# A four-batch attention and mixing kernel: the first batch's Fourier stage by head pairs, its channel stage by halves, the weight conversion re-timed

## Chip, cores and metric

The kernel runs on one core of one Trainium2 chip. The metric is device time in microseconds (us) of one execution; a profiled execution has a span besides, which is a little shorter than its time. PE is TensorE (PEld its weight loads), DVE is VectorE, ACT is ScalarE, POOL is GpSimd, SP is the engine that issues most DMAs.

## What is computed

Three blocks follow each other for four batches (8 heads, 576 tokens, head dimension 64, model width 512):

```python
# 1 attention with a learned decay, for each batch and head
scores = q @ k.T / 8 + cum[:, None] - cum[None, :]     # cum = cumsum(log f), causal
x = softmax(scores) @ v                                # heads joined: 576 x 512
# 2 Fourier mixing and a channel MLP of 2048 features
u = x + real(fft(fft(x, axis=tokens), axis=features))
un = (u - mean(u)) / sqrt(var(u) + 1e-6)
x = u + relu(un @ w_ch1) @ w_ch2
# 3 gated spatial MLP
h = relu(x @ w_in);  a, b = h[:, :512], h[:, 512:]
out = (a * (w_spatial @ norm(b) + b_spatial)) @ w_out
```

The weights arrive as 64-bit floats and are turned into pairs of 16-bit numbers (a high and a low part) on the chip. Every product is three matmul passes: high by high, high by low, low by high.

## The kernel before

**Stages.** Batch 0's attention and Fourier stage run alone at the start (`xfirst`, order in the list `START`). Then `mlp(b)` runs for each batch: `mlp1` is the channel MLP, `mlp2` the gated one. While `mlp(b)` runs, the attention and Fourier stage of batch b+1 (`xsteps`) is laid between its pieces: every piece of `mlp` yields a planned duration, and events with due times up to that point are emitted (`run`, L1176). The due times stand in the tables `LATER` and `SECOND`. In this part the order on PE is the order of emission; the other engines' orders are chosen by the scheduler from a timeline of its own. In `START` only SP's order is fixed by hand.

**Attention.** It goes by four head pairs. Each pair has `load`, `stack` (transposes of q and k, copies to 16 bits, DMAs into the operand tiles S1 and S2), `max` (row maxima, then `mc`, L576 to L583, which carries the negated maximum as two 16-bit numbers, transposed into S2), `score` (four groups of scores, exponentials, a high and a low part; `XPOOL` says for batch 0 which low parts POOL makes) and `pv` (the product with v, then the division that writes the pair's 128 columns of X).

**Fourier stage.** `fold_pair` adds and subtracts mirrored tokens on POOL as soon as a pair is done (L725). After the last pair `fold` does the same over mirrored features, twice, and `hilo` splits the result. `dft1` transforms over tokens (36 matmuls of 321 columns), `dft2` over features (36 matmuls of about 128 columns and 27 of one), then X is updated. `norm_tile` normalises one token tile of five, transposes it and splits it into `unT`, which `mlp1` reads. Tiles 0 and 1 are done in `START`, tiles 4, 3, 2 at due times from `NORM2`.

**Channel stage.** `mlp1` (L880) has 24 units: three token tiles of 192, and for each eight pairs of 128-feature groups. `first(u)` makes 24 matmuls from `unT` and W1, `second(u)` 24 from the result and W2, two units later. Token tile after token tile goes through all 2048 features, so that the first eight units need all of W1 and W2.

**Weights.** 44 blocks of 128 rows by 512 (`weight_list`: w0 to w15 for W1, w16 to w31 for W2, w32 to w39 for W_in, w40 to w43 for W_out). `load_w` (L333) takes each through a DMA of 512 KB into a ring slot, two ACT operations (L349, L351), two of DVE (L353, L354), a POOL product (L363), an ACT copy (L365) and a POOL subtraction (L366). For the blocks in `VSIGN` a third DVE operation (L358) stands for L351 and L363. Two pairs of temporaries are used in turn. `START` holds w0 to w15 in full and the DMAs of six later blocks; the other 28 blocks follow in `weights_left`, four blocks in each of the first three units of `mlp1(0)` and one in each later unit (`WSTEP`), then the spatial weights.

## Time and profile before

| what | value |
|---|---|
| median of 3 runs | 966.71 us (964.13 to 968.37) |
| profiled execution, its own time | 966.72 us |
| its span | 965.0 us |
| PE busy | 844.5 us (88%) |
| DVE, ACT, POOL busy | 595.8, 395.5, 267.0 us |
| mean granted PE clock | 0.941 of full |

The stages of the profiled execution, by the first matmul of each: batch 0's attention and Fourier stage 0 to 144.67 us; `mlp1(0)` 144.67 to 324.17; `mlp2(0)` to 397.73; `mlp1(1)` to 538.44; `mlp2(1)` to 613.38; `mlp(2)` to 812.98; `mlp(3)` to the end. The busy times are averages over stages that have different limits, so a stage is read by the stretches of busy time, clock and idle time in it, not by the totals of the table.

### The profile page before, as it was taken

How to read it: one execution, taken by the hardware profiler on the slowest of the kernel's cores; microseconds unless marked ns; L12 is line 12 of the kernel's file. 1: busy time of each engine (PE TensorE's matmuls, PEld its weight loads, DVE VectorE, ACT ScalarE, POOL GpSimd, SP SyncE). 2: the span in 40 equal slices, each digit the busy share in tenths (PEclk: the TensorE clock that was granted, in tenths of full speed). 3: DMA queues.
4: the chain of work that ended last, by engine and by line, in shares of the span. 5: the costliest groups of instructions: out<-in, count | busy, mean ns of one | idle time of the engine just before them, and what ended most of it. 6: DMA issues, size and time to landing. Idle time of an engine off the chain costs nothing.

```text
span 965.0 us, 22425 instructions
## 1 busy us (share of the span) xinstructions
PE 844.5 (88%) x9405; PEld 730.0 (76%) x9405; DVE 595.8 (62%) x1452; ACT 395.5 (41%) x694; POOL 267.0 (28%) x372
## 2 busy tenths in 40 slices
PE   3776336897899899899999999899999999999997
PEld 2655135787899677589999686699999587999874
DVE  4676878897854776575765865576574973133341
ACT  1856456766634244253334234243323334111132
POOL 4565888554610542000000550000000450000010
PEclk9897567898899999999999999999999999999999
DMA  6772336917220000622010003522100001000001
GB/s 150 211 234 76 115 97 171 224 42 189 93 59 18 20 2 21 159 63 64 5 36 2 1 2 74 122 58 63 38 3 2 1 2 44 2 2 2 1 1 55
DMA packets 75020, 60.89 MB, mean 63 GB/s; under 512 B 59869, under 2 KB 60263, under 8 KB 74791
## 3 DMA queue, kind: packets, MB, share of 16 engines
q1 hardware_dynamic: 74199, 58.13, 23.2%
q0 software_dynamic: 720, 1.33, 0.6%
q8 instruction: 74, 1.21, 0.5%
q14 instruction: 27, 0.22, 0.1%
HBM read 40.43 MB, written 4.83 MB: 47 GB/s over the span
## 4 chain that ended last, share of the span: by engine, by line
PE 58%; DVE 5%; DMA 2%; SPq 1%; issue 1%; ACT 1%; POOL 0%; ACTq 0%; DVEq 0%
PE ph L898 15%; PE acc L919 14%; PE vs L1063 6%; PE pu L990 5%; PE pvv L1004 4%; PE po L1081 3%; PE yps L778 1%; PE sc L619 1%; PE sc L623 1%; PE pv L686 1%; PE tr L869 1%; PE mxt L589 1%; PE pv L688 1%; PE pv L687 1%; DMA S<-a 1%; PE eo L811 1%
## 5 line engine op out<-in xcount | busy, mean ns | idle before, releaser
L898 PE MATMUL ph<-unT,W 128*128 128x192 f16 x2304 | 212.2, 250 | 5.1 <-DVE hT L905 2.7
L919 PE MATMUL acc<-hT,W 128*128 128x192 f16 x2304 | 205.3, 246 | 0.0
L898 PEld LDWEIGHTS <-W 128*128 128x128 f16 x2304 | 196.8, 100 | 11.2 <-issue 6.3
L919 PEld LDWEIGHTS <-W 128*128 128x128 f16 x2304 | 191.7, 98 | 0.1
L904 ACT ACTIVATE hT<-ph 128x384 f16<-128x384 f32 x96 | 46.9, 489 | 143.8 <-PE ph L898 143.4
L905 DVE SCALAR_TENSOR_TENSOR hT<-ph,hT 128x384 f16<-128x384 f32 x96 | 53.1, 553 | 82.3 <-ACT hT L904 82.1
L643 ACT ACTIVATE P<-sc 128x1024 f16<-128x1024 f32 (+1 forms) x64 | 53.8, 841 | 70.3 <-DVE sc L636 53.9
L657 DVE TENSOR_TENSOR P<-sc,P 128x1024 f16<-128x1024 f32 (+3 forms) x50 | 49.7, 993 | 30.1 <-ACT sc L655 29.1
L688 PE MATMUL pv<-vh,P 128*128 128x65 f16 (+2 forms) x480 | 59.3, 203 | 6.2 <-POOL P L653 6.2
L619 PE MATMUL sc<-S 128*128 128x256 f16 (+2 forms) x288 | 54.1, 249 | 10.8 <-DVE a L493 7.0
L686 PE MATMUL pv<-vh,P 128*128 128x65 f16 (+2 forms) x480 | 60.0, 205 | 2.9 <-DVE P L657 2.9
L976 POOL COPY tsc<-sc 128x2 f32<-128x2 f32 (+1 forms) x24 | 4.6, 213 | 206.8 <-DVE sc L948 206.5
L687 PE MATMUL pv<-vh,P 128*128 128x64 f16 (+2 forms) x480 | 59.3, 203 | 0.0
L495 POOL COPY a<-a 128x2 f16<-128x2 f16 x32 | 6.4, 207 | 187.1 <-ACT a L492 137.2
L1063 PE MATMUL vs<-WP,vn 128*128 128x288 f16 x448 | 56.5, 286 | 0.0
L623 PE MATMUL sc<-S 128*128 128x256 f16 (+2 forms) x288 | 55.1, 249 | 0.0
L688 PEld LDWEIGHTS <-P 128*128 128x128 f16 (+2 forms) x480 | 50.0, 110 | 6.7 <-POOL P L653 6.6
L1004 PE MATMUL pvv<-WI,unT 128*128 128x512 f16 (+1 forms) x240 | 54.7, 381 | 0.0
L687 PEld LDWEIGHTS <-P 128*128 128x128 f16 (+2 forms) x480 | 49.8, 110 | 3.5 <-issue 3.2
L686 PEld LDWEIGHTS <-P 128*128 128x128 f16 (+2 forms) x480 | 49.2, 108 | 3.6 <-issue 0.2
L1063 PEld LDWEIGHTS <-vn 128*128 128x128 f16 x448 | 43.6, 98 | 10.8
L990 PE MATMUL pu<-unT,WI 128*128 128x192 f16 x576 | 51.5, 250 | 0.0
(231 smaller groups left out, 1652.9 us busy)
## 6 DMA issues: line engine op xcount, KB each, us to landing
S<-a SPq DMA_DIRECT2D x96, 144.2 KB, 3.0
WI<-in_moe_w_ch_dram SPq DMA_DIRECT2D x16, 512.0 KB, 4.7
W<-in_moe_w_ch_dram SPq DMA_DIRECT2D x16, 512.0 KB, 4.3
a<-in_k_dram SPq DMA_DIRECT2D x32, 144.0 KB, 3.9
a<-in_q_dram SPq DMA_DIRECT2D x32, 144.0 KB, 3.7
vraw<-in_v_dram SPq DMA_DIRECT2D x16, 256.0 KB, 5.7
WP<-in_moe_w_in_dram SPq DMA_DIRECT2D x8, 512.0 KB, 3.6
out_dram<-ob SPq DMA_DIRECT2D x16, 256.0 KB, 2.9
```

The lines of the kernel that those rows point to most:

```text
L619: T.matmul(ps[:, j, c0:c0 + w], S2[s][:, j, QN + 128 * kt:QN + 128 + 128 * kt], qh, start=i == 0, stop=False,)
L623: T.matmul(ps[:, j, c0:c0 + w], S1[s][:, j, 128 * kt:128 * kt + 128], q1, start=False, stop=last and b not in PEMASK,)
L643: A.activation(out=pt[:, 0], in_=src, func=AF.Exp, scale=1.0 / 2048.0)
L686: T.matmul(ps[:n, j, o0:o0 + 65], hi, vh[:kk, 0, kt, h, :], start=(i == 0), stop=False)
L687: T.matmul(ps[:n, j, o0:o0 + 64], hi, vh[:kk, 1, kt, h, 0:64], start=False, stop=False)
L688: T.matmul(ps[:n, j, o0:o0 + 65], lo, vh[:kk, 0, kt, h, :], start=False, stop=(i == len(jobs) - 1),)
L898: T.matmul(ph[:, c, :], W1[:, a, kc, 128 * ff:128 * ff + 128], unT[:, e, kc, tok(t)], start=(c == 0 and kc == 0 and i == 0), stop=(c == 1 ...
L905: V.scalar_tensor_tensor(out=hT[:, 1], in0=ph, scalar=0.0, in1=hT[:, 0], op0=ALU.max, op1=ALU.subtract)
L919: T.matmul(acc[t][d // 2][:, d % 2, :], W2[:, a, ff, 128 * d:128 * d + 128], hT[:, e, c, :], start=(ff == 0 and i == 0 and d % 2 == 0), st ...
L990: T.matmul(ph[:, c, :], WI[:, a, kc, 128 * ff:128 * ff + 128], xT[:, e, kc, tok], start=(c == 0 and kc == 0 and i == 0), stop=(c == 1 and ...
L1004: T.matmul(pv[:n, :], xT[:, a, kc, 128 * i:128 * i + n], WI[:, e, kc, DM:2 * DM], start=(kc == 0 and j == 0), stop=(kc == 3 and j == 2),)
L1063: T.matmul(ps, vn[:kk, a, s, 128 * c:128 * c + 128], WP[:kk, e, s, tok], start=i == 0, stop=i == len(jobs) - 1,)
```

## The change

Six edits go together.

- **Fourier stage of batch 0 by head pairs.** `fold_pair` folds tokens in two operations (for pair 2 on DVE, else on POOL) and splits the result at once; `dft1_first` transforms a pair's 128 columns over tokens (18 matmuls of 321 columns for each pair, 72 in all); `dft2_first` transforms over features without a fold, by full tables of 257 and 255 columns (72 matmuls of about 256 columns), the first three pairs' part apart from the fourth's. The tables are 1 MB more of DMA, after `tab`.
- **Channel stage of batch 0 by halves.** `mlp1(0)` goes through three token tiles with 1024 features, then again with the other 1024. Six more additions to `uT` on DVE.
- **Weights.** The order of blocks is now w0 to w7 the first half of W1, w8 to w15 the first half of W2, w16 to w31 the second halves, then W_in and W_out. `START` holds w0 to w7 in full up to a mark `|`. The 180 steps of the other 36 blocks get due times from `WT`: steps 0 to 64 at -5.1 to 8.6 planned us of `mlp1(0)`, up to step 93 at 35.5, the last weight step at 87, then the 12 spatial steps. `VSIGN` has five blocks in place of three.
- **pv.** The division is three DVE operations over all five token tiles in place of twelve; the middle tile's matmuls use 128 columns of weights in place of 65.
- **mc.** Two DVE operations in place of three; the constant that they carried goes into the exponential's bias.
- **Due times.** `LATER`, `SECOND`, `NORM2`, `NORD` (tiles 2, 4, 3) and `XPOOL` (third low part of group 3 to DVE) have new values.

```diff
-R1, R2 = 4, 4
-VSIGN = (0, 1, 5)
+VSIGN = (0, 5, 14, 18, 43)
-WSTEP = (4, 3)
-NORM2 = (0, 2.838, 3.101)
+WT = ((0, -5.1), (64, 8.6), (93, 35.5), (198, 98.0))
+NORD = (2, 4, 3)
+NORM2 = (0.58, 3.602, 3.209)
-FOLDV = (1, 0, 1)
-XADDV = (4,)
+PARTV = (2,)
+XADDV = (0,)
-XPOOL = (3, 4, 4, 3)
+XPOOL = (3, 4, 4, 2)
...
+score3 w3 w2 score3 w3 w2 score3 part2 score3 score3 score3 tok2 w3 score3 score3 w2 score3 w2 w4
+w4 w4 score3 w4 w3 tok2 score3 score3 pv3 pv3 part3 w6 w5 w5 feat0 w5 w6 w6 part3 feat1 tok3 tok3
+feat0 w5 feat0 feat0 norm0 feat1 feat1 feat2 w7 w7 feat2 w7 norm0 feat2 feat1 w7 norm1 norm1 feat2
+norm0 w6 norm1 norm1 norm0 | w8 w16 w8 w8 w8 w13 w8 w18 w11 w9 w10 w17 w9 w12 w9 w9 w19 w10 w9 w15
...
-        mr = rp.tile([128, 2, 5], F32, name="mr", tag="mr")
-        V.tensor_scalar(
-            out=mr, in0=mcol, scalar1=-1.0 / 16384.0, scalar2=LOG16 * 2048.0 / 16384.0,
-            op0=ALU.mult, op1=ALU.add,
-        )
-        V.tensor_copy(mc[:, :, :, 30], mr)
-        V.tensor_tensor(mc[:, :, :, 31], mr, mc[:, :, :, 30], op=ALU.subtract)
+        V.tensor_tensor(
+            mc[:, :, :, 30], mcol, neg.unsqueeze(2).broadcast_to([128, 2, 5]), op=ALU.mult
+        )
+        V.scalar_tensor_tensor(
+            out=mc[:, :, :, 31], in0=mcol, scalar=-1.0 / 16384.0, in1=mc[:, :, :, 30],
+            op0=ALU.mult, op1=ALU.subtract,
+        )
...
+        po = ps[:, :, 0:325].rearrange("p j (t d) -> p j t d", d=65)
+        V.tensor_scalar(out=rc, in0=po[:, :, :, 64], scalar1=16.0e-9, scalar2=None, op0=ALU.add)
+        V.reciprocal(rc, rc)
+        V.tensor_tensor(
+            X[:, :, 2 * D * hp:2 * D * hp + 2 * D].rearrange("p t (j d) -> p j t d", j=2),
+            po[:, :, :, 0:64], rc.unsqueeze(3).broadcast_to([128, 2, 5, 64]), op=ALU.mult,
+        )
...
     def fold_pair(hp):
+        E = V if hp in PARTV else G
         c = slice(128 * hp, 128 * hp + 128)
+        for e, op in enumerate((ALU.add, ALU.subtract)):
+            E.tensor_tensor(XF0[:, e], X[:, 0:2, c], X[:, 4:2:-1, c], op=op)
+        yield
+        xh = XH0[hp % 2]
+        hilo(*(xh[:, o:o + 512].rearrange("p (e t n) -> p e t n", e=2, t=2) for o in (0, 512)), XF0)
+        r = len(TOK[2])
+        hilo(xh[:r, 1024:1152], xh[:r, 1152:1280], X[:r, 2, c])
+        yield
+    def dft1_first(hp):
+        xh = XH0[hp % 2]
+        p = xps("yps")
+        for eo, tb in enumerate((CT, ST)):
+            for t in range(3):
+                r = len(TOK[t])
+                for i, (a, e) in enumerate(PASSES):
+                    o = 512 * a + 256 * eo + 128 * t if t < 2 else 1024 + 128 * a
+                    T.matmul(p[:, eo, 0:321], xh[:r, o:o + 128], tb[e][:r, t, :],
...
+    def dft2_first(t):
+        for part in (range(3), range(3, 4)):
+            for k in part:
+                for eo, o, m in ((0, 0, 257), (1, 257, 255)):
+                    for i, (a, e) in enumerate(PASSES):
+                        T.matmul(p[:n, eo, eo:eo + m], YC0[:, k, a, eo, cs], TAB0[:, e, k, o:o + m],
...
+        ng = 2 if b == 0 else 1
+        nu = NFF // 2 // ng
+        units = [(g, t, nu * g + f) for g in range(ng) for t in range(3) for f in range(nu)]
...
+        nxt += [(float(np.interp(i, *zip(*WT))), f) for i, f in enumerate(wleft)]
```

## Rows read from the trace of the kernel before

**Rows 1.** The page: busy us, share of span, count; then the chain's shares
```profile
PE 844.5 (88%) x9405; PEld 730.0 (76%) x9405; DVE 595.8 (62%) x1452; ACT 395.5 (41%) x694; POOL 267.0 (28%) x372
PE 58%; DVE 5%; DMA 2%; SPq 1%; issue 1%; ACT 1%; POOL 0%; ACTq 0%; DVEq 0%
```

**Rows 2.** Stretches by stage: length, busy PE, PEld, DVE, ACT, POOL; clock, DMA share, GB/s
```profile
0.00:102.88 102.88, 59.68 (x721) 47.98 (x721) 66.59 (x143) 54.58 (x77) 57.64 (x66) 0.84 0.63 170
102.88:144.67 41.79, 16.05 (x115) 11.67 (x116) 33.90 (x70) 21.30 (x44) 36.66 (x40) 0.59 0.30 89
144.67:324.17 179.50, 156.45 (x1915) 146.47 (x1915) 133.21 (x261) 105.05 (x179) 84.94 (x88) 0.90 0.40 108
...
397.73:538.44 140.71, 135.08 (x1779) 128.54 (x1777) 90.73 (x268) 49.31 (x74) 4.29 (x16) 0.99 0.18 41
```

**Rows 3.** The same within `mlp1(0)`, and the first four units of `mlp1(2)` last
```profile
144.67:186.66 41.99, 28.72 (x244) 25.09 (x244) 35.38 (x52) 27.29 (x47) 30.22 (x28) 0.76 0.74 191
186.66:215.00 28.34, 26.97 (x375) 25.31 (x374) 28.02 (x53) 20.85 (x36) 15.38 (x13) 1.00 0.33 88
215.00:250.00 35.00, 27.34 (x292) 25.33 (x290) 25.10 (x49) 25.14 (x41) 19.68 (x20) 0.90 0.55 149
613.38:637.03 23.65, 23.05 (x250) 21.10 (x249) 17.84 (x49) 11.34 (x17) 0.37 (x2) 0.96 0.39 95
```

**Rows 4.** Stretches, line L366 alone (one for each converted weight block): POOL busy (count)
```profile
0.00:102.88 102.88, 8.12 (x6) 0.84 0.63 170
102.88:144.67 41.79, 9.48 (x8) 0.59 0.30 89
144.67:186.66 41.99, 13.61 (x11) 0.76 0.74 191
186.66:215.00 28.34, 5.95 (x6) 1.00 0.33 88
215.00:250.00 35.00, 10.29 (x9) 0.90 0.55 149
```

**Rows 5.** What PE waited for, 144.67 to 324.17 us: total us, times, longest
```profile
PE mxd L512 <- DMA S<-a: 7.0, 1, 7.0
PE mxt L589 <- DVE mc L583: 2.5, 1, 2.5
```

**Rows 6.** Timeline 95 to 141 us: start, us, engine, line, operation, count, idle before
```profile
95.72 0.16 DVE L696 TENSOR_SCALAR rc<-pv 128x4 f32<-128x4 f32 x1 [0.51 <-PE pv L688]
98.24 1.50 DVE L358 SCALAR_TENSOR_TENSOR WO<-W,WO 128x512 int32<-128x512 int32 x1
102.41 0.47 DVE L703 TENSOR_TENSOR X<-pv,rc 128x128 f32<-128x128 f32 x2
...
117.35 2.62 PE L778 MATMUL yps<-tab,xoh 128*128 128x321 f16 x9
123.65 0.82 DVE L785 SCALAR_TENSOR_TENSOR yc<-yps,yc 128x642 f16<-128x642 f32 x1
129.73 0.91 POOL L831 TENSOR_TENSOR X<-X,tt 128x256 f32<-128x256 f32 x1
140.34 1.09 PE L869 MATMUL tr<-cft,un 128*128 128x128 f32 x4 [12.19 <-DVE un L855]
```

**Rows 7.** Groups by line, of 144.67 to 324.17 us: busy us, mean ns
```profile
L388 PE MATMUL wpps<-cft,wps 128*128 128x128 f32 (+1 forms) x15 | 2.6, 273 | 0.0
L354 DVE SCALAR_TENSOR_TENSOR wt<-wt 128x512 int32<-128x512 int32 x4 | 2.8, 689 | 0.2
L354 DVE SCALAR_TENSOR_TENSOR WO<-WO 128x512 int32<-128x512 int32 x26 | 21.7, 840 | 2.8 <-ACT WO L349 2.6
L363 POOL TENSOR_TENSOR WO<-WO,W 128x512 f32<-128x512 f32 x18 | 24.0, 1335 | 20.0 <-DVE WO L354 11.2 <-DMA vraw<-in_v_dram 4.2 <-DVE mr L578 2.4
```

**Rows 8.** The same view for the mc line L582, 0 to 215 and 400 to 965 us
```profile
L582 DVE CAST mc<-mr 128x10 f16<-128x10 f32 x6 | 4.1, 679 | 0.2
L582 DVE CAST mc<-mr 128x10 f16<-128x10 f32 x8 | 1.5, 188 | 0.2
```

More of the change, by code (lines that the diff above doesn't have):

```diff
@@ L136 @@
+w41 w40 w40 w41 w41 w41 w43 w42 w42 w42 w42 w42 w43 w43 w43 w43
 """
@@ new lines, in dft2_first @@
+    def dft2_first(t):
+        X = state[0]["X"]
+        n = len(TOK[t])
+        cs = slice(128 * t, 128 * t + n)
+        p = xps("eo")
+        for part in (range(3), range(3, 4)):
+            for k in part:
+                for eo, o, m in ((0, 0, 257), (1, 257, 255)):
+                    for i, (a, e) in enumerate(PASSES):
+                        T.matmul(
+                            p[:n, eo, eo:eo + m], YC0[:, k, a, eo, cs], TAB0[:, e, k, o:o + m],
+                            start=k == 0 and i == 0, stop=k == 3 and i == 2,
+                        )
+            yield
+        es = rp.tile([128, 512], F32, name="es", tag="s2", bufs=NS2)[:n]
+        A.activation(out=es[:, 0:257], in_=p[:n, 0, 0:257], func=AF.Copy)
+        tt = rp.tile([128, 512], F32, name="tt", tag="s2", bufs=NS2)[:n]
+        for i, op in enumerate((ALU.subtract, ALU.add)):
+            V.tensor_tensor(tt[:, 256 * i + 1:256 * i + 256], es[:, 1:256], p[:n, 1, 1:256], op=op)
+        yield
+        for tl, a in ((t, 0), (4 - t, 1)) if t < 2 else ((2, 0),):
+            e = 1 - a
+            E = V if tl in XADDV else G
+            xt = X[:n, tl, :]
+            for xc, src in (
+                (slice(1, 256), tt[:, 256 * a + 1:256 * a + 256]),
+                (slice(511, 256, -1), tt[:, 256 * e + 1:256 * e + 256]),
+                (slice(0, 257, 256), es[:, 0:257:256]),
+            ):
+                E.tensor_tensor(xt[:, xc], xt[:, xc], src, op=ALU.add)
@@ L734, in fold @@
         r = len(TOK[t])
-        E = V if b == 0 and FOLDV[t] else G
+        E = G
         sp = state[b]["a"][:r]
@@ L828, in dft2 @@
             e = 1 - a
-            E = V if b == 0 and tl in XADDV else G
+            E = G
             xt = X[:n, tl, :]
@@ L952, in mlp1 @@
         todo = []
-        for u in range(3 * nu + 2):
-            if u < 3 * nu:
+        for u in range(len(units) + 2):
+            if u < len(units):
                 first(u)
@@ L1118, in xsteps @@
                 seqs[f"part{hp}"] = fold_pair(hp)
-        for t in range(3):
-            seqs[f"fold{t}"] = fold(b, t)
-        for c in range(2):
-            seqs[f"tok{c}"] = dft1(b, c)
-        for t in range(3):
-            seqs[f"feat{t}"] = dft2(b, t)
+                seqs[f"tok{hp}"] = dft1_first(hp)
+        if b:
+            for t in range(3):
+                seqs[f"fold{t}"] = fold(b, t)
+            for c in range(2):
+                seqs[f"tok{c}"] = dft1(b, c)
+        for t in range(3):
+            seqs[f"feat{t}"] = dft2(b, t) if b else dft2_first(t)
         for t in range(5):
@@ L1137, in at @@
                 t, n = t if isinstance(t, tuple) else (t, 1)
-                ev.append((t, lambda: [next(seqs[key]) for _ in range(n)]))
+                ev.append((t, lambda: [next(seqs[key], None) for _ in range(n)]))
         at("v", *L["v"])
@@ L1162, in xfirst @@
         seqs["decay"] = decay_rows()
+        seqs.update({"b" + k: g for k, g in second.items()})
         wl = weight_list()
@@ L1165, in xfirst @@
             seqs[f"w{i}"] = load_w(i, *w)
-        for key in START.split():
+        first, rest = START.split("|")
+        for key in first.split():
             next(seqs[key])
-        return seqs
+        return seqs, [lambda s=seqs[key]: next(s) for key in rest.split()]
     def mlp(b):
@@ L1179, in run @@
             evs.pop(0)[1]()
+    second = xsteps(1)
     with tc.manual_schedule(engines={mybir.EngineType.SP}):
-        left = xfirst()
-    def weights_left():
-        for i in range(28 + NFF):
-            if any(True for _ in [*left[f"w{i}"]]):
-                yield
-        yield from load_spatial()
-    lw = weights_left()
-    def wsteps(n):
-        for _ in range(n):
-            next(lw, None)
+        left, wleft = xfirst()
+    spatial = load_spatial()
+    wleft += [lambda: next(spatial, None)] * 12
     pool0.__exit__(None, None, None)
```

151 lines of the change are left out of this document (84 added, 67 removed), and 2 rows, old and new, of the table PV.

## The prediction

> **What bounds the kernel now.** I read the page's totals first, then stretches of busy time cut at the stages, then the same inside `mlp1(0)`, then the waits there and the timeline of the tail before it. The totals say PE: 844.5 of 965.0 us busy, and 58% of the chain that ended last is PE [rows 1]. The stages say where that holds. From `mlp1(1)` on PE has 135.08 of 140.71 us [rows 2], so there only less PE work would help. Up to 102.88 us (the last write of pair 3's attention into X) PE has 59.68 of 102.88. Between there and the first channel matmul at 144.67 it has 16.05 of 41.79 at a clock of 0.59, while POOL has 36.66 and DVE 33.90 [rows 2]: here the conversion of weights and the fold share POOL and DVE, and PE waits. `mlp1(0)` takes 179.50 us where `mlp1(1)`, with the same matmuls and no weights, takes 140.71 [rows 2]. Its first four units take 41.99 us against 23.65 for those of `mlp1(2)` [rows 3]. The change works on the first 324.17 us alone; the 73.56 of `mlp2(0)` (to 397.73, where the next stretch begins) and the 567.27 us behind it I leave as they are, since PE fills `mlp1` there [rows 2].
>
> **The attention of batch 0.** Added: three times 18 matmuls of `dft1_first` in front of pair 3. Nine of them take 2.62 us at the low clock [rows 6], so 18 take about 4.9, and 14.7 in all. PE is idle for 43 of 102.88 us [rows 2], which would hide all of it if it fell there; where it stands ahead of scores it delays the pair. I charge a fifth, 3 us; the ends are 0 and 10. The splits of parts (about 1.3 us of ACT and DVE for a pair) are paid by the shorter pv and mc. Conversions: before, 6 blocks are done by 102.88 us [rows 4]; after, w0 to w4 stand ahead of pv3 in `START`, so no more. The extra 1 MB of tables passes in about 5 us at the 190 GB/s of [rows 3] and falls behind `load2`; the DMA share of 0.63 [rows 2] leaves room, and its cost is 0 to 3 us. Removed: pair 3's division starts at 95.72 and ends at 102.88, because weight steps (L358, 1.50) and fold steps stand between its twelve operations [rows 6]. Three operations take about 1.2 us, so 97. With the 3 us, X is complete at about 100 (95 to 110).
>
> **The tail from X to the first unit.** Before, 41.8 us. After, step by step from [rows 6], for pair 3 alone: two POOL operations of 256 columns at 0.91, 1.8; split on ACT and DVE with the middle rows, 1.8; 18 matmuls, 4.9; two copies of 0.82 or a little less, 1.5; the fourth pair's part of two `feat` steps, 12 matmuls of 256 columns, by columns from the same 2.62 about 2.7 (the other three pairs' parts run while PE waits); `es` and `tt`, about 1.2; additions to X on POOL for tiles 4 and 1, five of 0.91 or less, 4.7 at most; statistics, a power, `un`, eight transposes at 1.09 for four, and the split, 5.8 (an estimate but for the transposes). That sums to 24.4. On the same engines three blocks are still to be converted (w5 to w7) in place of eight [rows 4]; a block is about 2.5 us of POOL and 1.5 of DVE [rows 7]. Some ten hand-overs that each meet half an operation of 0.8 to 1.3 us cost about 5. So 29 us (24 to 36), and the first unit starts at 129 in place of 144.67: 15.7 gained. The fold's DVE and POOL operations disappear with this; they were on the path, so what is late next is the token transform on a cold PE and POOL's additions.
>
> **`mlp1(0)`.** Its PE work at full clock: 135.1 as in `mlp1(1)`, plus transposes of three token tiles, about 5 [rows 6], plus 2.6 of spatial transposes [rows 7]: 143. The halves add no matmul; they add six additions on DVE, about 3 us. So before, 36.5 of 179.5 us are lost: 23.05 idle and 13.5 to the lower clock. The head (four units) loses 18.3 of it [rows 3], the rest 18.2. No wait for a converted block is among PE's; its waits are those of batch 1's attention, above all 7.0 for the operands' DMA and 2.5 for mc [rows 5], each queued behind weight steps on DVE, ACT or POOL.
> After, 36 blocks are left in place of 30. In the head, 64 steps, or 12.8 blocks, fall due before 8.6 planned us; before, 12 blocks in the first three units. The head is therefore not relieved: the same stack, DMA and maxima stand between its first two units. I take 16, two less for the shorter mc. In the rest, 23 blocks: six thinly over seven units, then 17 at 1.3 for a unit of 5.4 us (140.71 / 26), one in 4.1 us. At one in 4.7 us (6 blocks in 28.34) PE lost 1.4 us, 0.23 a block [rows 3, 4]; at one in 3.9 (9 blocks in 35.00) 7.7 idle and some 2.7 by clock, 1.2 a block [rows 3, 4]. Six at 0.23 and 17 at about 0.55 make 11. Load agrees: DVE has 133.2 plus 9 for six more blocks, 3 for additions, 2 for `VSIGN`, less 8 for pv and mc, 139 of 170, or 82%; it had 84% in the head and 99% up to 215 [rows 3]. So 143 + 16 + 11 = 170, against 179.5. Bounds: 151, if only the 7.0 and little else stays; 185, if the rest pays 18.2 times 23/19. The moved DMAs share SP's queue with the attention's operand DMAs: a weight DMA that waits for its slot holds those behind it, which is inside the 7.0 and 16 taken. POOL has 84.9 plus 15 less 4, 96 of 170, and is no bound.
>
> **Edits with one answer.** The middle tile's pv matmuls stream the same 65 columns, so their wider weights cost nothing. `XPOOL` moves one subtraction of about 0.8 us from POOL to DVE, both idle then for part of the time. The new due times of batches 1 to 3 move work that lies beside a full PE; I take 0, with 5 either way, and in those batches pv and mc shorten DVE only, which has 90.73 of 140.71 us there [rows 2].
>
> **A rule against it.** The mc operation L582 takes 0.679 us up to 215 us, while POOL is busy, and 0.188 after 400 [rows 8]; L354 takes 0.840 and 0.689 [rows 7].
> The Trainium skill, page "SBUF — State Buffer", section "Who interferes with whom", says that DVE and GpSimd share a port pair: a DVE operation with two inputs in SBUF waits for a whole GpSimd operation that reads SBUF, as does a copy in its fast mode. By that rule the two new mc operations, each with two SBUF inputs, can still be held, the head gets back nearer 1 us than 2, and closer packing lengthens DVE's own steps. The trace agrees with the lengthening; that the new form is held no run here shows yet.
>
> **Sum.** 129 + 170 + 73.6 + 567.3 = 939.9 us of span. The profiled execution's own time is 966.72, 1.7 over its span, and equal to the median of 966.71, so 941.6.
>
> **Rivals.**
> 1. *The spreading works fully.* Rest and head lose only 12: 155; X at 97 with the same tail, 126. 126 + 155 + 73.6 + 567.3 + 1.7 = 923.6. For it: 186.66 to 215 lost 1.4 us with six blocks and DVE full [rows 3]. Against it: 64 steps due at once.
> 2. *DVE and POOL crowd each other.* Six more blocks in the stage cost at the old price: 185 in place of 170, 956.6. For it: the lengthened L354 [rows 7], and 215 to 250 us, where nine blocks cost PE 10.4 [rows 3]. That rule of the Trainium skill would give the same.
> 3. *Slower: the units wait for their blocks.* The place is `second` of the second half, which needs w31, 24 blocks after the first unit, with nine units behind it. At r us for a block and a start 5 us early, the stage is 24r - 5 + 9 x 5.41. It reaches the 195.2 that undoes the gain of 15.7 at r = 6.3, and is slower by over 0.5% from 6.5; at 6.7 it is 204.5, and the time 976. Against it: 41.99 us for 11 blocks is 3.8, 28.34 for 6 is 4.7 [rows 4].
> 4. *No change: the tail doesn't shorten.* If the token transforms and eight blocks push pair 3 to 110 and the tail to 30, the first unit comes at 140; with 184 the time is 966.6.
>
> **How the numbers follow.** The forecast (928 to 954) has 0.52, rival 1 0.20, rival 2 0.16, rival 3 0.06, rival 4 0.06. Faster by over 0.5% (under 961.9; 0.5% is about what a measurement of this kernel can tell from no change) is the forecast, rival 1 and most of rival 2: 0.86. Same: rival 4 and the slow end of rival 2, 0.08. Slower: rival 3, 0.06. The range leaves out 0.06 below (a tail at its lower end together with rival 1) and 0.14 above: 914 to 961.
>
> **What would show it.** Right: the first `ph` matmul at 120 to 136 us; between X and it 24 to 36 us with about three L366; 36 L366 after it; the first four units in 36 to 42 us; the first `pvv` of batch 0 290 to 308 us in; the distance from there to the end within 5 us of 640.8. Wrong: PE waits named after L366 or L365 (rival 3); a first unit after 138 (rival 4); L354 over 0.9 us on average with a stage over 180 (rival 2); a head near 24 us (rival 1). The prediction fails most easily in the head, for which I took the old loss because the same steps crowd into it.

## The result, and the profile of the changed kernel

The changed kernel takes 973.25 us (median of 5 runs, 970.67 to 975.85) where the kernel before took 966.66 beside it (964.13 to 968.37): a ratio of 1.0062 with a 95% interval of 1.0033 to 1.009. The change makes it 0.6% slower. I had forecast 941.6 us in a range of 914 to 961.

The page's totals of the changed kernel answer [rows 1]:

```profile
span 974.1 us, 22331 instructions
PE 855.5 (88%) x9450; PEld 735.8 (76%) x9450; DVE 576.1 (59%) x1283; ACT 408.5 (42%) x693; POOL 258.6 (27%) x357
```

DVE has 169 instructions and 20 us less than before, as the diff says, and POOL 8 us less. PE has 11 us more, and 974.1 - 855.5 = 118.6 us idle against 120.5 before. So work was taken from the two engines that I had called crowded, and the span still rose by 9.1 us, nearly what PE got.

The stages follow, cut at the landmarks that the prediction used (last write of pair 3 into X, first `ph`, first `pvv` of batch 0, first `ph` of batch 1). They answer [rows 2]; the columns are the length of the stretch, each engine's busy time and instructions, the granted clock as a share of full speed, the DMA share and GB/s.

```profile
0.00:118.25 118.25, 74.08 (x801) 58.37 (x802) 77.23 (x121) 71.33 (x102) 67.30 (x70) 0.83 0.64 170
118.25:152.24 33.99, 13.81 (x83) 10.52 (x80) 22.75 (x43) 13.89 (x26) 24.40 (x30) 0.63 0.46 142
152.24:336.33 184.09, 156.79 (x1924) 145.63 (x1924) 127.72 (x235) 106.28 (x183) 82.36 (x90) 0.92 0.36 93
336.33:405.86 69.53, 64.74 (x520) 45.42 (x518) 45.10 (x113) 27.27 (x59) 22.59 (x44) 0.98 0.18 38
```

| stretch | before | forecast | after | after less forecast |
|---|---|---|---|---|
| attention of batch 0, to X complete | 102.9 | 100 | 118.25 | +18.25 |
| tail, X to the first unit | 41.8 | 29 | 34.0 | +5.0 |
| `mlp1(0)` | 179.5 | 170 | 184.1 | +14.1 |
| `mlp2(0)` and all behind it | 640.8 | 640.9 | 637.8 | -3.1 |
| span | 965.0 | 939.9 | 974.1 | +34.2 |

The attention gives 15.4 us more than before, `mlp1(0)` 4.6 more; the tail gives back 7.8 and the rest 3.1. That is the whole 9.1 us between the two profiled executions. So the question is why the attention got longer, and why the stage of the halves didn't get shorter.

**The attention.** PE's busy time up to X rose from 59.68 us [rows 2] to 74.08, by 14.4. Its idle time went from 43.2 to 44.2. The new PE work (9.1 us of `yps` matmuls and 3.0 of `eo` in that stretch) lay on top of the old idle time, none of it inside; and the 184 score matmuls take 22.8 us together in place of 18.3. PE's waits up to X in the kernel before, then in the changed one, say why; the columns are what waited for what, us in total, times, and the longest.

```profile
PE mxt L589 <- DVE mc L583: 9.6, 3, 4.7
PE mxd L512 <- DMA S<-a: 6.8, 2, 6.4
PE pv L688 <- POOL P L653: 6.2, 2, 5.6
PE pk L482 <- DMA a<-in_k_dram: 6.2, 2, 5.2
```

```profile
PE yps L773 <- ACT W L746: 14.6, 3, 7.2
PE mxt L629 <- DVE mc L620: 7.1, 3, 3.5
PE mxd L552 <- DMA S<-a: 5.8, 1, 5.8
PE pk L522 <- DMA a<-in_k_dram: 5.2, 1, 5.2
```

The longest entry of the changed kernel is new: three token transforms (L773) wait 14.6 us for the split of their pair (L746). The timeline around the first of them shows the queue at work (rows of PE, POOL, ACT and DVE; start, duration, and in brackets how long the engine sat idle and for what).

```profile
48.73 0.24 PE L728 MATMUL pv<-vh,P 128*128 128x65 f16 x1
...
49.95 0.82 DVE L737 TENSOR_TENSOR X<-pv,rc 128x640 f32<-128x640 f32 x1 [0.53 <-DVE rc L736]
...
51.28 1.45 POOL L755 TENSOR_TENSOR W<-X 128x256 f32<-128x256 f32 x2
...
54.36 0.67 ACT L388 ACTIVATE WO<-W 128x512 f32<-128x512 f32 x1 [3.24 <-DMA W<-in_moe_w_ch_dram]
...
55.47 0.63 ACT L746 ACTIVATE W<-W 128x512 f16<-128x512 f32 x1
...
56.16 0.72 PE L773 MATMUL yps<-tab,W 128*128 128x321 f16 x2 [7.18 <-ACT W L746]
...
56.67 0.37 PE L659 MATMUL sc<-S 128*128 128x193 f16 x1
```

Pair 0 is divided at 50.77, and POOL has its part done at 52.73. The split could start then, but in ACT's queue a weight step (L388) stands ahead of it and waits 3.24 us for its DMA. PE finished pv at 48.97, has the transform of pair 0 next in its queue, and stands for 7.18 us; behind it stand scores of pair 1 (L659), which then start without a wait of their own. The exponential of that group follows at 58.72.

The queue of ACT is the smaller part of the wait. Of the 7.18 us 1.8 pass until the division is done, 2.0 on POOL's part, 2.7 in ACT's queue and 0.7 on the split. The other two waits end at 75.75 (3.55 us) and 106.59 (3.82), and no step that waits for a DMA stands in them. The second has the split right behind POOL's part; in the third two exponentials stand ahead of the split for 1.5 us (rows of POOL, ACT and DVE):

```profile
73.62 1.41 POOL L755 TENSOR_TENSOR W<-X 128x256 f32<-128x256 f32 x2 [1.02 <-DVE X L737]
...
75.06 0.63 ACT L746 ACTIVATE W<-W 128x512 f16<-128x512 f32 x1 [0.31 <-POOL W L755]
...
102.72 1.71 DVE L755 TENSOR_TENSOR W<-X 128x256 f32<-128x256 f32 x2
...
105.91 0.63 ACT L746 ACTIVATE W<-W 128x512 f16<-128x512 f32 x1
```

So some 4 of the 14.6 us are the queue on ACT. The rest is the chain itself, division, fold and split, which PE sees in full because the transform follows its own pair at once.

**The blocks.** L405 ends the conversion of a block, as L366 did in [rows 4]; L405 by stretch (length, POOL busy and count, clock, DMA share, GB/s):

```profile
0.00:118.25 118.25, 11.95 (x10) 0.83 0.64 170
118.25:152.24 33.99, 7.36 (x6) 0.63 0.46 142
152.24:336.33 184.09, 34.01 (x28) 0.92 0.36 93
```

I had forecast at most 6 in the attention, 3 in the tail and 36 in the stage. It is 10, 6 and 28.

**`mlp1(0)`.** The first four units take 38.63 us, inside the 36 to 42 of the forecast. What the forecast doesn't have is the end of the stage. Its last 24.09 us in the changed kernel, and then the last 24.09 us of the same stage before:

```profile
312.24:336.33 24.09, 17.91 (x217) 15.94 (x216) 13.32 (x44) 9.09 (x28) 10.71 (x24) 0.79 0.14 37
```

```profile
300.08:324.17 24.09, 24.09 (x349) 23.77 (x347) 12.15 (x37) 8.47 (x22) 5.82 (x11) 1.00 0.10 26
```

PE is idle for 6.2 of 24.09 us there where it was full before, and its clock is 0.79 in place of 1.00. The timeline of PE in the changed kernel shows what stands there: four runs of spatial transposes (L427) close behind each other, with a wait for DVE ahead of the scores before them and ahead of three of the four.

```profile
318.40 0.19 PE L659 MATMUL sc<-S 128*128 128x65 f16 x1 [1.89 <-DVE WP L434]
...
319.20 0.49 PE L427 MATMUL wpps<-cft,wps 128*128 128x128 f32 x3
321.78 0.62 PE L427 MATMUL wpps<-cft,wps 128*128 128x128 f32 x2 [2.09 <-DVE P L697]
323.29 1.33 PE L427 MATMUL wpps<-cft,wps 128*128 128x128 f32 x5 [0.89 <-DVE WP L434]
325.93 0.58 PE L427 MATMUL wpps<-cft,wps 64*128 64x64 f32 x3 [1.31 <-DVE WP L434]
```

Before, the same transposes came one group every 2.3 to 6.5 us from 301.9 to 342.0 us, between units and the first steps of `mlp2(0)`.

### The profile page after: what moved, and what is told of

Same layout as the page of the kernel before. It is cut to its first block, busy times and chain, and to the rows that moved or that the text cites. A ratio compares the mean times of both kernels' runs of the same rounds, so it can differ in the third digit from the quotient of the medians.

```text
span 974.1 us, 22331 instructions
## 1 busy us (share of the span) xinstructions
PE 855.5 (88%) x9450; PEld 735.8 (76%) x9450; DVE 576.1 (59%) x1283; ACT 408.5 (42%) x693; POOL 258.6 (27%) x357
## 4 chain that ended last, share of the span: by engine, by line
PE 66%; DVE 14%; DMA 6%; ACT 6%; issue 3%; POOL 3%; SPq 2%; DVEq 0%; ACTq 0%; POOLq 0%
PE ph L989 16%; PE acc L1011 15%; PE vs L1158 6%; PE pu L1085 5%; PE pvv L1099 3%; PE po L1176 3%; PE pv L726 2%; DMA W<-in_moe_w_ch_dram 2%; PE sc L659 2%; DVE mcol L574 1%; PE mxt L629 1%; DMA S<-a 1%; PE tr L957 1%; PE sc L663 1%; DMA WP<-in_moe_w_in_dram 1%
## 5 line engine op out<-in xcount | busy, mean ns | idle before, releaser
L683 ACT ACTIVATE P<-sc,log 128x1024 f16<-128x1024 f32 (+1 forms) x64 | 59.4, 928 | 103.6 <-DVE sc L676 79.9
L697 DVE TENSOR_TENSOR P<-sc,P 128x646 f16<-128x646 f32 (+3 forms) x51 | 50.4, 989 | 46.4 <-ACT sc L695 46.3
L659 PE MATMUL sc<-S 128*128 128x256 f16 (+2 forms) x288 | 56.9, 257 | 9.7 <-DVE mcol L567 3.2
L726 PE MATMUL pv<-vh,P 128*128 128x65 f16 (+2 forms) x480 | 58.5, 204 | 2.5 <-DVE a L533 2.1
L663 PE MATMUL sc<-S 128*128 128x256 f16 (+2 forms) x288 | 58.8, 257 | 0.0
L728 PE MATMUL pv<-vh,P 128*128 128x65 f16 (+2 forms) x480 | 57.5, 202 | 0.0
L1099 PE MATMUL pvv<-WI,unT 128*128 128x512 f16 (+1 forms) x240 | 56.7, 392 | 0.0
L726 PEld LDWEIGHTS <-P 128*128 128x128 f16 (+2 forms) x480 | 47.5, 104 | 7.2 <-DVE a L533 2.4
L1085 PEld LDWEIGHTS <-WI 128*128 128x128 f16 x576 | 49.6, 101 | 1.4 <-issue 0.8
L728 PEld LDWEIGHTS <-P 128*128 128x128 f16 (+2 forms) x480 | 48.6, 106 | 0.7 <-issue 0.6
```

The source lines that it names most:

```text
L659: T.matmul(ps[:, j, c0:c0 + w], S2[s][:, j, QN + 128 * kt:QN + 128 + 128 * kt], qh, start=i == 0, stop=False,)
L663: T.matmul(ps[:, j, c0:c0 + w], S1[s][:, j, 128 * kt:128 * kt + 128], q1, start=False, stop=last and b not in PEMASK,)
L683: A.activation(out=pt[:, 0], in_=src, func=AF.Exp, scale=1.0 / 2048.0, bias=log16)
L726: T.matmul(ps[:n, j, o0:o0 + 65], hi, vh[:kk, 0, kt, h, :], start=(i == 0), stop=False)
L728: T.matmul(ps[:n, j, o0:o0 + 65], lo, vh[:kk, 0, kt, h, :], start=False, stop=(i == len(jobs) - 1),)
L1085: T.matmul(ph[:, c, :], WI[:, a, kc, 128 * ff:128 * ff + 128], xT[:, e, kc, tok], start=(c == 0 and kc == 0 and i == 0), stop=(c == 1 and ...
```

## The experiments

Theory A: a pair's token transform stands in PE's queue ahead of the next pair's scores and waits there for a split that is late. Theory B: the blocks converted early, inside the attention and the tail, make these longer. Theory S: the spatial steps came to stand in a bunch. Theory O came up on the way: the order in which the scheduler fills the queues of ACT, DVE and POOL is worth as much as any part of the change. All ratios are to runs of the kernel before on the same chip beside it, with their 95% interval; the other columns are from the profiled execution of each kernel, in us. One execution is a draw, too: the profiled one of tok_late took 982.85 us and that of tok_two_spatial 971.87, both 8 over their medians, that of tok_two 960.94, 3 under; and `mlp2(1)`, which the edit of tok_two doesn't touch, took 68.42 us in the changed kernel and 66.76 in tok_two.

| kernel | median | ratio | X complete | first `ph` | `mlp1(0)` |
|---|---|---|---|---|---|
| the kernel before | 966.7 | 1 | 102.9 | 144.7 | 179.5 |
| the changed kernel | 973.3 | 1.0062 (1.0033 to 1.0090) | 118.25 | 152.2 | 184.1 |
| pv_alone | 975.0 | 1.0079 (1.0055 to 1.0104) | 102.9 | 150.3 | 180.4 |
| halves_alone | 971.9 | 1.0050 (1.0025 to 1.0075) | 105.5 | 152.2 | 177.1 |
| four_alone | 976.7 | 1.0082 (1.0058 to 1.0106) | 129.9 | 163.9 | 172.9 |
| div_only | 976.3 | 1.0105 (1.0067 to 1.0142) | 101.4 | 149.2 | 183.6 |
| mc_bias_only | 974.6 | 1.0085 (1.0052 to 1.0118) | 108.2 | 157.7 | 173.3 |
| before_vsign | 974.4 | 1.0077 (1.0048 to 1.0105) | 102.7 | 148.2 | 184.8 |
| before_vsign2 | 971.0 | 1.0029 (1.0008 to 1.0050) | 101.4 | 145.7 | 184.6 |
| before_gate | 973.5 | 1.0083 (1.0057 to 1.0109) | 104.8 | 139.0 | 191.9 |
| after_gate | 985.9 | 1.0208 (1.0179 to 1.0236) | 118.5 | 148.5 | 197.7 |
| after_vsign | 981.1 | 1.0138 (1.0099 to 1.0177) | 122.7 | 158.6 | 183.5 |
| tok_late | 974.6 | 1.0062 (1.0036 to 1.0089) | 123.6 | 156.6 | 184.3 |
| tok_two | 964.1 | 0.9982 (0.9955 to 1.0010) | 112.65 | 145.1 | 179.9 |
| tok_two_vsign | 967.5 | 0.9993 (0.9971 to 1.0015) | 110.6 | 145.3 | 184.8 |
| tok_two_gate | 972.6 | 1.0074 (1.0047 to 1.0101) | 109.0 | 137.2 | 199.0 |
| tok_two_conv | 966.6 | 0.9989 (0.9971 to 1.0006) | 112.6 | 149.0 | 184.3 |
| after_spatial | 967.9 | 1.0001 (0.9977 to 1.0024) | 117.9 | 150.2 | 177.2 |
| after_spatial_vsign | 975.5 | 1.0077 (1.0048 to 1.0107) | 124.1 | 157.9 | 176.0 |
| tok_two_spatial | 964.1 | 0.9962 (0.9941 to 0.9983) | 113.6 | 147.8 | 179.8 |

### Each part alone, on the kernel before

**pv_alone**: the diff's edits to `attn_pv`, mc, the exponentials and `XPOOL`, nothing else.

> The kernel before with one part of the change alone: the middle token tile's pv matmuls with 128 columns, the division in three operations for all five tiles, mc in two operations on mcol, log 16 as the exponential's bias, and XPOOL's last entry 2. Fourier stage, channel stage and weight order stay as before. What I thought in the prediction: the division of pair 3 gets some 6 us shorter, so X is complete at about 97 in place of 102.88, and 960 to 964 us follow. Rival: the operations only change places with weight steps on the same engines, X stays at 102 to 104 and the time within 2 us of 966.7. Rival: the bias makes every exponential 0.09 us longer and ACT decides, 968 to 970.

1.0079: slower, and not in the stretch that I had named. X is complete at 102.9 as before; the tail takes 47.4 us in place of 41.8, with ten blocks converted in it in place of eight.

**div_only** and **mc_bias_only** take that part apart.

```
div_only:      only the PV table's third row (65 -> 128) and the division in three operations
mc_bias_only:  only neg, log16, mc in two operations and bias=log16
```

> The kernel before with the wider middle pv and the division in three operations alone (log 16 stays in mc's four operations). If pv_alone's 7 us come from the bias or mc: 960 to 967 us, X at 97 to 103. If they come from the division: 972 to 976 us.

> The kernel before with mc in two operations on mcol and log 16 as the exponential's bias alone; division and pv as before. If the bias (each exponential 0.09 us longer, 64 of them on the way to the end of mlp1(0)) or the two-input mc operations cost pv_alone its 7 us: 971 to 976 us. If not: 963 to 968 us. If each part by itself reshuffles the scheduler's order at a loss: both this and div_only over 969.

Each is slower by as much as both together (1.0105, 1.0085 and 1.0079), though div_only only replaces twelve DVE operations by three and widens one operand of pv. Two separate causes of 7 us should have added up. This is the case I had written last in the expectation of mc_bias_only, that any edit reshuffles the order at a loss. It became theory O.

**halves_alone**: the halves and the weight list in that order; START without the early DMAs of w18, w19, w32 and w33, and each later block's DMA two blocks ahead.

```diff
+            work = any(True for _ in [*left[f"w{i}"]])
+            if 16 <= i < 26 + NFF:
+                next(left[f"w{i + 2}"], None)
```

> The kernel before with the channel stage of batch 0 in halves of 2048 features and the weight list in that order, the blocks still converted one for each unit (four for each of the first three), each block's DMA two blocks ahead. Fourier stage, pv and mc as before. If the halves by themselves relieve mlp1(0): first unit unchanged at 143 to 147, the stage 170 to 175 in place of 179.5, 957 to 962 us. If the head with batch 1's stacks and maxima sets the stage and not the blocks' dates: the stage 177 to 182, 964 to 969 us. If the units wait for blocks at the second half: over 185, over 972 us.

1.0050. The stage takes 177.1, at the edge of the second case; the tail took 5.0 us more than before. The halves by themselves don't relieve the stage by the 9.5 us I had forecast; 2.4 is what the profile shows, with 29 blocks in the stage in place of 30.

**four_alone**: the Fourier stage by pairs in the kernel before.

```diff
-... pv0 w18 stack2 stack2 max1 pv0 max1 score1 score1 ...
+... pv0 w18 stack2 max1 pv0 max1 part0 part0 stack2 score1 tok0 tok0 score1 ...
```

> The kernel before with the Fourier stage of batch 0 by head pairs (parts, token transforms placed among the scores as in the changed kernel, no fold over features), the rest as before; w32 and w33 are fetched at the end of START, since their slots hold the transformed pairs. Theory A (a pair's 18 token matmuls stand in PE's queue ahead of the next pair's scores and wait there for POOL's parts and the split): X complete at 111 to 118, first unit at 144 to 152, 966 to 974 us. Theory B (what made the attention longer in the changed kernel is the ten blocks converted inside it, not the token transforms): X at 101 to 106, first unit at 131 to 138, 952 to 960 us.

1.0082, with X at 129.9, outside theory A's 111 to 118 and far from theory B's 101 to 106. PE waits three times for a split here as well, 16.8 us in all. Of the parts this one alone moves X far, by 27.0 us; pv_alone moves it by 0.0, halves_alone by 2.6. But ten blocks are converted before X, too, so this run doesn't clear theory B of its share. The tail (34.0) and the stage (172.9) are 7.8 and 6.6 us shorter than before.

### Where the order comes from: edits without work

The scheduler fills the queues anew for every kernel. So three kernels change only which block gets its sign on DVE.

```diff
before_vsign    -VSIGN = (0, 1, 5)            +VSIGN = (0, 1, 6)
before_vsign2   -VSIGN = (0, 1, 5)            +VSIGN = (0, 2, 5)
after_vsign     -VSIGN = (0, 5, 14, 18, 43)   +VSIGN = (0, 4, 14, 18, 43)
```

> The kernel before with VSIGN (0, 1, 6) for (0, 1, 5): the sign of block 6 in place of that of block 5 goes to DVE, no work is added or removed, PE's order is the same, and the scheduler puts ACT, DVE and POOL in another order in some hundred rows. Theory O (the order before is a favourable one among many near it, and any edit that reshuffles it costs 3 to 9 us): 970 to 976 us. Rival (the parts themselves cost): 964 to 969 us.

> The same with VSIGN (0, 2, 5): again no change of work; here PE's order changes too. Theory O: 970 to 977 us. Rival: 964 to 969 us.

> The changed kernel with VSIGN (0, 4, 14, 18, 43) for (0, 5, 14, 18, 43): no change of work, the queues reshuffled. If the changed kernel's order is as favourable as any near it: 973 to 982 us. If its 973 is a common draw: 966 to 980, either side, which would make the 0.6% between the two kernels a matter of the order drawn.

All three are slower than the kernel that they change: before_vsign by 0.77%, before_vsign2 by 0.29%, and after_vsign with 1.0138 against 1.0062. In before_vsign X comes at 102.7 as before; the tail took 3.7 us more and the stage 5.3. The order of either kernel is a favourable one among its neighbours, and a new draw costs about 3 to 8 us. Theory O is shown to that extent. It means that the losses of 0.5 to 1.05% of the parts alone can't be laid to the parts, and that the 0.6% between the two kernels is itself no larger than a draw. What moves by more, or moves the same way under two orders, can still be told.

### Theory B: the early blocks

**before_gate**, **after_gate**: w8 to w15 can't be fetched before the tail's first feature step.

```diff
+            if 8 <= i < 16:
+                V.tensor_copy(slot[:, 0:1], gate.bitcast(I32))
             nc.sync.dma_start(slot, src)
```

`gate` is a column that DVE copies from that step's result (from `y1` before, from `es` after).

> The kernel before with one edit: the DMA of each of w8 to w15 waits for a one-column DVE copy that needs the first feat step of the tail, so these eight blocks can't be converted ahead of it. Theory B (blocks that nobody needs yet stand in the queues of ACT, DVE and POOL ahead of the attention's and the tail's steps; 14 of them are done by the first unit, though it needs four): the tail shrinks from 41.8 us by 6 to 12, the first unit comes at 133 to 139, mlp1(0) pays some of it back, the whole 957 to 965 us. Theory A (the token transforms in PE's queue are what went wrong in the change): nothing here concerns them, the first unit stays at 143 to 147, and mlp1(0) gets longer by up to 8, 966 to 975 us.

> The changed kernel with the same gate on w8 to w15 (at the first es of the tail). Theory B: X complete at 108 to 114 in place of 117.4 (two blocks fewer inside the attention), the tail 24 to 29 in place of 34, first unit at 133 to 142, the whole 960 to 968 us. Theory A: X at 115 to 119, the tail 31 to 34, the whole 969 to 975 us.

Stretches of before_gate, then of after_gate (X, tail, stage):

```profile
0.00:104.78 104.78, 60.11 (x721) 48.21 (x721) 66.62 (x142) 53.02 (x74) 56.95 (x66) 0.86 0.57 152
104.78:139.00 34.22, 13.50 (x116) 10.50 (x117) 28.14 (x70) 14.49 (x31) 24.05 (x30) 0.65 0.41 127
139.00:330.90 191.90, 159.82 (x1915) 148.21 (x1915) 137.14 (x272) 114.37 (x194) 98.91 (x97) 0.87 0.39 107
```

```profile
0.00:118.46 118.46, 73.62 (x811) 56.88 (x811) 68.68 (x111) 63.05 (x88) 59.63 (x64) 0.87 0.51 126
118.46:148.50 30.04, 13.42 (x71) 10.18 (x72) 16.05 (x44) 10.47 (x20) 14.08 (x21) 0.68 0.55 194
148.50:346.20 197.70, 163.16 (x1925) 150.12 (x1925) 144.62 (x251) 118.23 (x203) 100.71 (x105) 0.88 0.40 107
```

Half of theory B holds: the tail shrinks, by 7.6 us and by 4.0. X doesn't move (118.46, though two blocks fewer lie ahead of it). And the stage pays more than the tail gave: 12.4 us with five blocks more in before_gate, 13.6 with seven more in after_gate; in tok_two_gate, below, 19.1 with seven. In before_gate this is no price of converting: PE's second products wait 10.0 us for blocks that come late, a wait that the kernel before doesn't have.

```profile
PE acc L924 <- ACT W L368: 7.4, 2, 5.5
PE acc L924 <- POOL W L369: 2.6, 2, 1.3
```

In after_gate and tok_two_gate no unit waits for a block, and the stage pays 1.9 and 2.7 us for each block more. So before_gate has theory B's first unit and theory A's time, and after_gate, at 985.9, lies above both. To fetch these eight blocks late is a loss on all three kernels.

**tok_two_conv** asks the same inside the attention: tok_two (below) with the DMAs of w0 to w4 behind the last stack.

> tok_two with the DMAs of w0 to w4 behind the last stack of batch 0, so that no block is converted in the first two pairs. If the blocks make the pairs longer: pair 1's write at 61 to 66 in place of 70, X at 103 to 108 in place of 112.6, the tail up to 8 longer, the whole within 4 of 964. If the token transforms' own work does it: X at 110 to 114.

Pair 1 comes at 65.7 in place of 70.0, as expected of the blocks; but by pair 3 it has all come back, X at 112.56 against 112.65, though eight blocks lie ahead of it in place of ten, and the time is 0.9989 against 0.9982. That is the second case: X follows the token transforms' own work. The two blocks lie in the tail now, which takes 36.4 us in place of 32.5.

### Theory A: the token transforms in PE's queue

**tok_late** moves the `tok` steps of pairs 0 to 2 in START to just ahead of the next pair's pv; **tok_two** moves `tok0` behind the scores of pair 2, `tok1` behind those of pair 3 and `tok2` behind pv of pair 3.

```diff
tok_two:
-... score1 w1 tok0 tok0 score1 ... max2 tok1 w5 tok1 score2 ... score3 tok2 w3 ... tok2 score3 score3 pv3 pv3 part3 ...
+... max3 tok0 tok0 pv2 max3 pv2 ... score3 score3 tok1 tok1 pv3 pv3 tok2 tok2 part3 ...
```

> The changed kernel with one edit: the token transforms of pairs 0, 1 and 2 stand one pair later, ahead of the next pair's pv and behind its scores; the same work, weights as they were. Theory A (PE's queue stands behind a token transform whose split is late): X complete at 103 to 109 in place of 117.4, the whole 960 to 967 us. Theory B (the ten blocks converted in the attention): X stays at 114 to 118, the whole 971 to 975 us.

> The changed kernel with the token transform of pair 0 behind the scores of pair 2, that of pair 1 behind the scores of pair 3, that of pair 2 behind pv of pair 3: the split of each is then some 20 us old. Theory A: PE's waits for a split (15.5 us in the attention) fall under 4 us, X complete at 104 to 109, the tail 1 to 4 us longer, the whole 963 to 969 us. Theory B: the waits move to scores and pv, X at 113 to 118, the whole 970 to 976 us.

tok_late gained nothing: 1.0062, as the changed kernel, and X at 123.6 is outside both ranges. Its trace has a reason: one pair's scores are too short a way. POOL has the part of pair 0 done at 52.08, but the split's step L746 comes at 59.42, behind weight steps and four exponentials on ACT, and PE, done at 51.46 with the scores and maxima ahead of it, waits 8.7 us for it in front of pv of pair 1. Such waits up to X sum to 12.1 us in place of 14.6, and those for mc to 16.7 in place of 7.1. tok_two goes further. PE's waits up to X in tok_two:

```profile
PE mxt L629 <- DVE mc L620: 13.2, 3, 7.5
...
PE yps L773 <- DVE P L697: 5.2, 2, 3.5
```

No transform waits for a split any more up to there (5.2 us are waits that end with a P subtraction of DVE); part of it went to the next link, mxt for mc (7.1 to 13.2). X comes at 112.65, 3.7 us after my expected 104 to 109, and the time is 964.1, within the expected 963 to 969. Of the 15.0 us between the two profiled executions 5.6 lie in the attention, 1.5 in the tail, 4.2 in the stage, and 3.7 behind it, where the edit moves nothing.

**tok_two_vsign** repeats it under the order of after_vsign.

> tok_two under the reshuffled order of after_vsign (VSIGN 0, 4, 14, 18, 43), to be held against after_vsign (981.1 us, 1.0138 of before). If the token transforms' place is a cause of its own: 6 to 12 us under it, 969 to 975 us, and PE's waits for a split in the attention under 4 us. If tok_two's gain was a favourable draw: 977 to 983 us.

967.5 us: 0.9993 against after_vsign's 1.0138. PE's waits for a split from 40 to 125 us, in after_vsign and then in tok_two_vsign:

```profile
PE yps L773 <- ACT W L746: 20.2, 4, 7.0
```

```profile
PE yps L773 <- ACT W L746: 2.0, 1, 2.0
```

So moving the transforms up to two pairs later gains 0.8% under one order and 1.4% under another, X comes 5.6 and 12.1 us earlier, and the wait that theory A names is gone or nearly so in both, while edits without work only lost. By these two pairs of runs the place of the transforms is a cause. How much of the gain is the new draw is open.

**tok_two_gate** has both this and the gate.

> Both edits together. If A and B each hold a part: X at 98 to 105, the tail 25 to 31, first unit at 124 to 135, the whole 948 to 960 us. If only one of them acts, no better than the better of the two alone. If neither, 969 to 976 us.

1.0074: X comes at 109.0, 3.7 us before tok_two's, with two blocks fewer ahead of it; the tail is down to 28.2 us and the first unit at 137.2, and the stage takes 199.0. What the gate adds to tok_two is a loss, as on the other two kernels.

### Theory S: the spatial steps

**after_spatial** and **after_spatial_vsign** give the twelve spatial steps later due times.

```diff
-WT = ((0, -5.1), (64, 8.6), (93, 35.5), (198, 98.0))
+WT = ((0, -5.1), (64, 8.6), (93, 35.5), (180, 87.3), (192, 121.0))
```

> The changed kernel with the dates of the twelve steps for the spatial weights alone changed: one every 2.8 planned us up to 121 in place of all by 94, so that their transposes lie among the last channel units and the first steps of mlp2(0), as before the change. Theory S (the steps came to stand in a bunch at the end of the stage, where PE has 13.82 of 20 us at a clock of 0.74): mlp1(0) 175 to 179 in place of 184.1, mlp2(0) up to 3 longer, the whole 964 to 969 us. Rival (PE would wait there anyway, for batch 1's attention): within 2 of 973.

> after_spatial under the same reshuffled order. If the bunch of spatial steps is a cause of its own: 4 to 7 us under after_vsign, 974 to 977 us. If it was a draw: 979 to 983 us.

967.9 us, 1.0001 against 1.0062, and under the other order 1.0077 against 1.0138: 0.6% each time. The stage shrinks by 6.9 and 7.5 us, and `mlp2(0)` takes 3.1 and 3.3 more. The last 24.09 us of the stage in after_spatial, beside the row of the changed kernel above:

```profile
303.30:327.39 24.09, 19.81 (x279) 19.09 (x277) 13.80 (x37) 7.13 (x17) 5.47 (x10) 0.93 0.05 14
```

PE is busy for 1.9 us more and its clock is 0.93 in place of 0.79. For the changed kernel theory S holds under both orders.

**tok_two_spatial** has both cures.

> Token transforms two pairs later (as in tok_two) and the spatial steps spread (as in after_spatial). If theories A and S are separate: 9 less from A and 5 to 8 from S, 954 to 960 us, faster than both kernels. If S is no cause: 962 to 966 us.

964.1 us, 0.9962 (0.9941 to 0.9983): the only kernel here that is faster than both, by 0.4% than the one before. It isn't the 954 to 960 that two separate gains would give. From tok_two (0.9982) it can't be told apart. The last 24.09 us of the stage in tok_two, then in tok_two_spatial:

```profile
300.94:325.03 24.09, 17.77 (x231) 16.03 (x230) 13.53 (x44) 10.41 (x32) 10.64 (x24) 0.86 0.13 37
```

```profile
303.47:327.56 24.09, 19.82 (x278) 19.04 (x277) 13.74 (x37) 7.17 (x17) 5.47 (x10) 0.93 0.05 14
```

So the end of the stage is relieved here as in after_spatial. But the stage as a whole takes 179.8 us in place of 179.9, in an execution that was 8 us over its median where tok_two's was 3 under; I have no run that says where the gain went.

## Why the prediction was wrong

**The token transforms.** "I charge a fifth, 3 us" was the step that failed worst. I took 43 us of idle PE for room. The idle time was there [rows 2], but it was made of waits (above all 9.6 us for mc, 14.2 for DMA and 8.2 for the subtractions behind the exponentials), each ahead of a step that the next one needs, and the transforms were put on that chain. PE's busy time to X rose by 14.4 us and idle time by 1.0: nothing was hidden. That 14.4 comes close to the 14.7 that I had added up is luck: the transforms took 9.1, the rest is feature steps and slower scores. "The ends are 0 and 10" didn't hold the result of 15.4 either. Two pairs later (tok_two) the wait for a split is gone, and X still comes 9.8 us later than before, with 12.7 us more of PE and 3.0 less idle. So 5.6 of the 15.4 went with the place of the transforms. The other 9.8 stayed; no run has the transforms with only the six blocks of the kernel before, so what part of it the blocks have is open.

**The splits of parts.** "Paid by the shorter pv and mc" counts busy time. The split is 1.3 us of work, but with the division and the fold it is a hand-over for which PE stands in front of each transform, 14.6 us in all, some 4 of them because other steps are ahead of it in ACT's queue. I had written of waits behind weight steps for `mlp1(0)` and not for this place.

**The blocks in the attention.** "w0 to w4 stand ahead of pv3 in `START`, so no more" read START as the order of all engines. It orders the DMA issues; the scheduler filled DVE, ACT and POOL with more blocks as soon as their data were there. Ten were done by X. What two of them cost the attention was little: with eight X stayed where it was in after_gate and tok_two_conv, and came 3.7 us earlier in tok_two_gate.

**The division.** Three operations, 116.7 to 118.25, 1.55 us for the 1.2 forecast: right. But the 5.9 us that the sum took off for it (102.88 to 97) are a third of the miss of 18.25, and they didn't come on the kernel before either: from the last pv matmul to X it is 3.6 us in pv_alone and 2.6 in div_only in place of 7.2, while that matmul itself ends 3.6 and 3.2 us later.

**The tail.** 34.0 for 29. I had three blocks in it and six were. With one block in it the runs gave 30.0 (after_gate) and 28.2 (tok_two_gate): five blocks fewer took off 4.0 and 4.3 us, some 0.8 each. So the count of blocks was a term that failed, and by that price half of the 5.0 us; the other half isn't placed. In four_alone nine blocks lie in a tail of 34.0. No mark of the 1 MB of tables shows: PE's waits for DMA up to X are 5.8 and 5.2 us, 6.8 and 6.2 before.

**`mlp1(0)`.** The head was right (38.63 us in 36 to 42). The rest was to lose 11 us; it lost 145.5 - (143 - 23.65) = 26. Two terms failed. The 11 for the rest has no spatial bunch, which I had counted as 2.6 us of matmuls and not placed: with the steps spread the stage was 6.9 and 7.5 us shorter. And the price of a block, 0.23 to 1.2 us, was read from stretches that held other work too; seven blocks more in the stage cost 1.9 each in after_gate and 2.7 in tok_two_gate. That price is for blocks that came due in the first units, and a gain per block by spreading the later ones was never seen: with 28 blocks instead of the forecast 36, the stage was longer than before. How the 26 us divide between the two no run shows. The upper bound of 185 held by luck: its own terms, 143 + 16 + 18.2 times 23/19, come to 181, and the stage took 184.1.

**What lies behind.** From the first `pvv` to the end 637.8 us, within 5 of 640.8: right.

**The rivals.** The fourth, "the token transforms and eight blocks push pair 3 to 110", had the right mechanism, and 0.06. Its size was too small in the attention and its stage of 184 was right. I gave it little because I looked for idle time in totals and not for what stands behind the transform in PE's queue. The third, units that wait for blocks, isn't what happened: no wait of PE in the stage names L405 or L404. It is what happened in before_gate.

**The rule against it.** The two new mc operations, in the changed kernel up to 215 us, and the second of them after 400 (duration min/median/max, first and last start):

```profile
L617 DVE TENSOR_TENSOR mc<-mcol,neg x5: 184/201/570, 21.1 to 175.7; 128x10 f16<-128x10 f32 x5
...
L620 DVE SCALAR_TENSOR_TENSOR mc<-mcol,mc x5: 203/1049/1152, 21.3 to 177.6; 128x10 f16<-128x10 f32 x5
...
L620 DVE SCALAR_TENSOR_TENSOR mc<-mcol,mc x8: 192/200/205, 420.1 to 723.0; 128x10 f16<-128x10 f32 x8
```

The second (L620) takes 0.20 us where POOL is quiet and 1.05 to 1.15 in the three places where POOL works; the first (L617) met a working POOL once, for its 0.57. PE's mxt waits 7.1 us for L620 up to X (9.6 for mc before). The Trainium skill, page "SBUF — State Buffer", section "Who interferes with whom", says that a DVE operation with two inputs in SBUF contends with a GpSimd operation that reads SBUF, and that the one that issues first holds the shared ports for its whole length. The trace agrees: at 69.84 a POOL operation of the conversion (L402) starts, 0.06 us ahead of L620, and runs 1.16 us; L620 takes 1.15 and ends 0.05 behind it. The change took an operation off DVE there but kept two that can be held.

**How far the verdict reaches.** The changed kernel is 0.6% slower than the kernel before in the orders that both were given. Since edits without work cost 0.3 to 0.8%, the sign of that difference isn't a property of the change alone. What is shown is that it doesn't bring the 2.6% I had forecast, and two places where it loses, the token transforms behind their own pair and the bunch of spatial steps.

## What to carry to other kernels

Idle time of an in-order engine is room only for work whose inputs are surely there: before work is moved into it, read what will stand behind it in the queue, and trace its inputs through the other engines' queues, at the head of which a step may wait for a DMA. A conversion that must be done somewhere is paid for where it goes: taken out of the tail here it gave some 0.8 us back and cost the next stage 1.9 to 2.7, so count what a move takes from one stretch and adds to the next. And where a scheduler fills the queues anew, measure an edit without work first: here it moved the time by 0.3 to 0.8%, and a gain counted only when it came back under a second order.
